# Sliding-window attention with an adaLN and SwiGLU block: the row-maximum products take 64 queries of both heads by a block-diagonal operand

## The chip, the cores and the metric

The kernel runs on one core of one Trainium2 chip. The metric is device time in microseconds (us) of one execution, from runs of the compiled program on the chip. A core has TensorE (PE, with its weight loads listed as PEld), VectorE (DVE), ScalarE (ACT), GpSimd (POOL) and SyncE (SP), which here only issues transfers; 16 DMA engines move the data.

## The reference

One transformer block on x of 2048 rows by 512, in float32. A vector c gives six modulation rows. Cut to what matters:

```
mod = silu(c) @ w_mod                       # sa, ca, ga, sb, cb, gb
h = layernorm(x) * (1 + ca) + sa
q, k, v = h @ wqkv                          # 32 heads of 16
scores = q @ k.T * 16 ** -0.5               # key index in (query - 256, query]
x = x + ga * (softmax(scores) @ v) @ wo
h = layernorm(x) * (1 + cb) + sb
out = x + gb * ((silu(h @ w1) * (h @ w3)) @ w2)
```

The softmax is over a window of 256 keys that ends at the query itself. This case is about the maximum over those keys, which is subtracted ahead of the exponential.

## The kernel before

**Tiling.** The sequence is cut into 4 blocks of 512 positions (`NB`, `BT`), the 32 heads into 8 groups of four (`NQ`). A unit is one group on one block, so there are 32 units, numbered u = 4 g + b. A unit's four heads are two pairs: index `a` picks one, and `hh` the head within it. Values that need more than one product's precision are held as high and low parts, so a projection is three products per chunk of 128 rows.

Each unit goes through three functions, and the three work on different units at the same time:

- `unit_a` (line 442) computes queries and keys: 12 products of 512 columns (line 451) into one bank `pj`, three ScalarE copies out of it (lines 457, 460 and 463), and two subtractions on GpSimd (`mix`, line 469) that leave three parts of each value. Then six transfers of 128 KB (`rows`, line 474) put the parts into `ring`, the operand memory in which one head's values have 48 rows (16 elements by three parts) and two heads have 96.
- `unit_b` (line 491) finds the row maximum: 16 products (line 504), each of 128 queries of one head against up to 384 keys. The stationary operand holds both heads' query rows (96 by 128), and the keys come from a copy of `ring` in which the other head's rows are zero. For each product VectorE adds the mask `mskq` and takes the maximum (line 511) and reads the accumulator. Then come `parts` (lines 519 and 520), a transpose (line 526), a ScalarE copy (line 531), and two small transfers `ring<-mT` (line 535) that put the negated maxima into extra rows of the query operand, so that the score product subtracts them itself.
- `unit_c` (line 743) makes 16 score products with keys as the stationary operand and up to 384 queries as columns (line 763), masks and exponentiates them, and multiplies by the values into the bank `po` (`values_of`, line 739). `MODE` gives each of the eight (key block j, pair a) one of the ways to mask: C merges the two partly masked blocks on VectorE (line 781), takes the exponential of 256 columns (line 784) and zeroes what is outside on GpSimd (line 791); D adds the mask on VectorE (line 771) and takes the exponential of 384 columns (line 775); P copies two blocks to a tile `sm` on ScalarE (line 798), takes the exponential of the free block (line 800), masks on GpSimd (line 808) and takes the exponential of the rest (line 812).

Score, row-maximum and projection products have three, three and one PSUM bank; `po` has one.

**Order.** Nothing is scheduled by the compiler. Every step is put on a list with a time, and each engine gets its steps in the order of those times; an engine does them in that order and waits where an operand is not there. The times are in slots: unit u begins at slot 8 u, `unit_a` of unit u at 8 (u - 3) + `oa`, `unit_b` at 8 (u - 2) + `ob`, and the dictionary `X` holds each step's place within its function. In every unit's eight slots there are therefore the projections of one unit, the maxima of an earlier one and the probabilities of one before that. SP also issues a store of the output bank (line 831), the loads and stores of a side job for the later feed-forward weights (lines 893 and 894; GpSimd does its arithmetic), and in every fourth unit the load of the next group's projection weights (line 432, split on lines 436 and 440) and a gate row (line 875).

Ahead of the units stand the modulation, the layer norm and the values of all blocks, with the first units by the plain times `Y`. The last units are merged by a planner (`Sched`) with the output projection and the feed-forward, which is TensorE products from end to end.

Of the kernel before, what the change touches and what calls it, by code (L numbers as in the profile page):

```python
# [17 lines left out]
H, DH = 32, 16  # L18
# [11 lines left out]
X = dict(oa=-1.228, ob=1.317, wqk=(-2.382, 3.131, 4.551), pj=(-1.966, -1.918, -1.881, -0.877, -0.359, -0.355,  # L30
         -0.265, 0.076, 1.497, 3.335, 3.917, 4.363), ev=(4.727, 5.775, 5.259), mix=(5.588, 6.021),
         row=(8.681, 8.806, 9.018), mx=(0.546, 0.669, 1.455, 2.0, 2.064, 2.307, 2.929, 2.957, 3.255, 4.081,
         4.688, 5.039, 6.139, 6.215, 6.787, 7.106), tl=(0.31, 0.576, 0.39, 0.716, 0.354, 0.742, 0.497, 1.151,
         0.762, 0.785, 0.491, 0.953, 0.338, 1.726, 1.317, 1.105), mr=(8.575, 8.773, 9.063, 9.269), st=(1.873,
         1.594, -2.503, 2.891, 0.05, 3.409, 2.644, 3.504, 4.618, 4.477, 4.419, 5.916, 5.311, 7.665, 6.691,
         6.671), c=(0.385, 0.805, 2.402, 0.573, 0.759, 1.126), pv=(4.115, 8.948, 9.091, 9.582, 3.792, 4.101),
         o=(9.93, 10.63), job=(-0.855, 2.493, 10.058))
Y = dict(wqk=(0, 4, 5), pj=(0.0, 0.382, 0.764, 1.146, 1.528, 1.91, 2.292, 2.674, 3.056, 3.438, 3.82, 4.202),
         ev=(4.991, 4.614, 4.813), mix=(5.389, 5.444), row=(5.416, 5.471, 6.776), mx=(0.0, 0.5, 1.0, 1.5,
# [3 lines left out]
MODE = 'CDCPCCCP'  # L43
# [259 lines left out]
def block_kernel(ctx: ExitStack, tc: tile.TileContext, x, wqk, wv, wo, w13, w2, c, wmod, out):  # L303
# [5 lines left out]
    ident = cst.tile([P, P], F32, name="ident")  # L309
    make_identity(nc, ident)  # L310
    nhalf = cst.tile([P, 4], F32, name="nhalf")
    nc.gpsimd.memset(nhalf, -0.5)
    o32 = cst.tile([P, P], F32, name="o32")
    nc.gpsimd.memset(o32, 1.0 / 32)
    odd = cst.tile([P, 1], F32, name="odd")

    def fill_odd():

        for hh in range(2):
            r = slice(64 * hh, 64 * hh + 64)  # L320
            nc.vector.tensor_reduce(
                out=odd[r], in_=ident[r].rearrange("p (c o) -> p c o", o=4)[:, :, 2 - 2 * hh:4 - 2 * hh],
                op=ALU.add, axis=mybir.AxisListType.XY)
        nc.vector.tensor_copy(identr, ident)
# [61 lines left out]
    ring = ap.tile([P, 3, 2, S], F32R, name="ring")  # L386

    NS, NM = 6 * DH, 6 * DH + 4

    def queries(rows, a, b, n):  # L390
        return ring[:rows, 1, a, b * P:(b + n) * P]

    def keys(rows, hh, a, b, n):
        return ring[:rows, 2 - 2 * hh, a, b * P:(b + n) * P]


    mskq = ap.tile([P, 3 * P], F32, name="mskq")
    nc.gpsimd.memset(mskq, 0.0)
    nc.gpsimd.affine_select(out=mskq[:, :P], in_=mskq[:, :P], pattern=[[1, P]], base=0,
                            channel_multiplier=-1, compare_op=ALU.is_gt, fill=NEG)  # L400
    nc.gpsimd.affine_select(out=mskq[:, 2 * P:], in_=mskq[:, 2 * P:], pattern=[[-1, P]], base=0,
                            channel_multiplier=1, compare_op=ALU.is_ge, fill=NEG)
    mskw = a1.tile([P, KC, P], F32, name="wqr", bufs=1)
    mskk = mskw[:, :2]
# [7 lines left out]
    identr = ap.tile([P, P], F32R, name="identr")  # L412
# [7 lines left out]
    def ring_fill(b, hh):  # L420
        k = ring.bitcast(F32)[:, 2 - 2 * hh, :, b * BT:(b + 1) * BT]
        nc.gpsimd.memset(k[:NM] if hh == 0 else k[:NS], 0.0)
        if hh:
            nc.gpsimd.memset(k[NS:NM], 1.0)
        nc.gpsimd.memset(k[NS:NS + 2], 1.0 - hh)
# [16 lines left out]
    def unit_a(u, t0, at, y=X):  # L442
# [11 lines left out]
        def out(n):  # L454
            if n == 0:
                v["raw"] = a1.tile([P, BT], F32, name="qkr", bufs=1)
                nc.scalar.activation(v["raw"], v["ps"], AF.Copy)  # L457
            elif n == 1:
                v[0] = a1.tile([P, BT], F32R, name="qk0", bufs=1)
                nc.scalar.activation(v[0], v["ps"], AF.Copy)  # L460
            else:
                v[1] = a1.tile([P, BT], F32R, name="qk1", bufs=1)
                nc.scalar.activation(v[1], v["ps"], AF.Copy, scale=odd)

        def mix(n):

            if n == 2:
                v[2] = a1.tile([P, BT], F32R, name="qk2", bufs=1)
            nc.gpsimd.tensor_tensor(out=v[n], in0=v["raw"], in1=v[1].bitcast(F32), op=ALU.subtract)  # L469

        def rows(r):
            rf = ring.bitcast(F32)
            for hh in range(2):
                nc.sync.dma_start(
                    rf[3 * hh + r:NS:6, 1 - hh:3 - hh, :, b * BT:(b + 1) * BT].rearrange(
                        "p x a t -> p (x a) t"),
                    v[r].bitcast(F32)[64 * hh:64 * hh + 64, :])
# [10 lines left out]
        for r in range(3):  # L488
            at(t0 + y["row"][r], lambda r=r: rows(r), "qk_rows")

    def unit_b(u, t0, at, y=X):
# [4 lines left out]
        def scores(i):  # L496
            qb, a, hh = i // 4, i // 2 % 2, i % 2
            gq = 4 * b + qb
            k0 = max(0, gq - 2)
            n = (gq + 1 - k0) * P  # L500
            if i == 0:
                v["mt"] = a1.tile([P, 2, 2, 4], F32, name="mt", bufs=2)
            v[i] = psA.tile([P, BT], F32, name="mx", bufs=MXB)
            nc.tensor.matmul(v[i][:, :n], queries(NS, a, gq, 1), keys(NS, hh, a, k0, gq + 1 - k0),  # L504
                             start=True, stop=True)

        def top(i):
            qb, a, hh = i // 4, i // 2 % 2, i % 2
            n = min(3, 4 * b + qb + 1) * P
            junk = a1.tile([P, 3 * P], BF16, name="junk", bufs=2)  # L510
            nc.vector.tensor_tensor_reduce(  # L511
                out=junk[:, :n], in0=v[i][:, :n], in1=mskq[:, 3 * P - n:], scale=1.0, scalar=-3e38,
# [1101 lines left out]
```

## Time and profile before

| | |
|---|---|
| runs | 969.67, 972.69 and 973.76 us; median 972.69 us |
| the profiled execution, first to last instruction | 971.3 us, 1.4 us under that median |
| TensorE busy | 942.4 us, of it the row-maximum products 154.9 us and the score products 155.3 us |
| VectorE busy | 734.9 us, of it the maximum over the row-maximum products 256.3 us |
| ScalarE and GpSimd busy | 557.1 and 538.2 us |
| DMA | 80672 packets, 141.65 MB |

Busy times are sums over instructions; on TensorE they overlap, since a product starts before the one ahead of it has drained. How far apart products start is therefore read from the chain of work that ended last, in which neighbours on one engine are counted from start to start. A line that starts with "L504 PE" is one group of instructions: line of the kernel, engine, operation, what is written and read, shapes and count, then busy time, mean duration in ns, and idle time ahead of them with its releaser.

### The profile page before, as it was taken

The page shows a single profiled execution, that of the slowest core. Times are in us where ns is not written, and L with a number is a line of the kernel's source. Part 1 is how long each engine was busy: PE and PEld are TensorE (multiplying, and loading weights), DVE is VectorE, ACT ScalarE, POOL GpSimd, SP SyncE. Part 2 cuts the span into 40 slices and gives each one's busy share as a digit, 9 for nine tenths or more (in the row PEclk, how much of TensorE's full clock was granted, in tenths as well). Part 3 has the DMA queues.
Part 4 walks back from the last instruction along what each step waited for, and adds up shares of the span by engine and source line. Part 5 has one row for each costly group of instructions (what it writes and reads, how often), then busy time and mean ns, then how long its engine had stood idle before and what let it go on. Part 6 is the DMA issues. An engine that isn't in the chain of part 4 may idle for free.

```text
span 971.3 us, 17150 instructions
## 1 busy us (share of the span) xinstructions
PE 942.4 (97%) x5316; PEld 717.5 (74%) x5316; DVE 734.9 (76%) x2034; ACT 557.1 (57%) x1258; POOL 538.2 (55%) x740
## 2 busy tenths in 40 slices
PE   6999999999999999998998999999999999999998
PEld 3678777777767776775577888888887888888886
DVE  7575889998989998999278686666679766677545
ACT  3333878787878787876578843433456343433330
POOL 8321777787868786865546765337759332222320
PEclk9999999999999999999898999999999999999999
DMA  9521354444544444435795564467654433222102
GB/s 317 170 77 36 134 182 143 144 143 144 176 143 143 144 144 143 133 128 174 211 243 139 194 217 151 142 206 249 194 195 165 141 119 94 63 65 72 44 23 87
DMA packets 80672, 141.65 MB, mean 146 GB/s; under 512 B 9538, under 2 KB 22338, under 8 KB 80580
## 3 DMA queue, kind: packets, MB, share of 16 engines
q1 hardware_dynamic: 79860, 139.50, 44.6%
q10 hardware_dynamic: 720, 1.05, 0.3%
q8 instruction: 42, 0.69, 0.3%
q14 instruction: 50, 0.41, 0.1%
HBM read 85.72 MB, written 34.61 MB: 124 GB/s over the span
## 4 chain that ended last, share of the span: by engine, by line
PE 83%; POOL 5%; DVE 4%; DMA 3%; issue 2%; ACT 2%; SPq 1%; POOLq 0%; DVEq 0%; ACTq 0%
PE st L1384 13%; PE mx L1384 11%; PE pj L451 7%; PE mx L504 7%; PE mx L1478 7%; PE st L763 7%; PE st L1478 7%; PE po L739 6%; PE pj L1384 5%; PE st L671 3%; PE pj L1478 2%; PE mx L1120 2%; POOL pt L791 2%; PE st L1120 2%; POOL qk L469 2%
## 5 line engine op out<-in xcount | busy, mean ns | idle before, releaser
L511 DVE CUSTOM_DVE_ANT_0 junk<-mx,mskq 128x384 bf16<-128x384 f32 (+2 forms) x512 | 256.3, 527 | 28.8 <-PE mx L504 27.2
L504 PE MATMUL mx<-ring 96*128 96x384 f32 (+2 forms) x512 | 154.9, 340 | 6.0 <-DMA ring<-qk 2.4
L763 PE MATMUL st<-ring 100*128 100x384 f32 (+2 forms) x512 | 155.3, 345 | 2.2 <-ACT pt L784 1.2
L791 POOL TENSOR_SCALAR_AFFINE_SELECT pt<-pt 128x256 f32<-128x256 f32 x268 | 109.3, 411 | 63.1 <-ACT pt L784 52.5
L451 PE MATMUL pj<-hT,wq 128*128 128x512 f32 x384 | 136.2, 404 | 1.2 <-DVE wq L440 0.8
L504 PEld LDWEIGHTS mx<-ring 96*128 96x128 f32 x512 | 93.5, 189 | 39.7 <-DVE mt L511 25.8
L784 ACT ACTIVATE pt<-st 128x256 f32<-128x256 f32 x268 | 96.1, 386 | 41.8 <-DVE st L781 33.8
L763 PEld LDWEIGHTS st<-ring 100*128 100x128 f32 x512 | 95.5, 190 | 23.7 <-issue 8.4
L739 PE MATMUL po<-pt,vS 128*17 128x384 f32 (+2 forms) x1408 | 98.6, 398 | 1.7 <-POOL pt L791 1.0
L469 POOL TENSOR_TENSOR qk<-qkr,qk 128x512 fp32r<-128x512 f32 x64 | 83.3, 1302 | 27.6 <-ACT qkr L457 27.4
L976 POOL TENSOR_TENSOR w<-w,w 128x512 fp32r<-128x512 f32 (+2 forms) x36 | 59.8, 1679 | 62.0 <-ACT w L975 44.6
L1428 POOL TENSOR_TENSOR t<-t,t 128x512 f32<-128x512 f32 x28 | 39.7, 1418 | 93.5 <-DVE t L1416 91.7
L781 DVE COPY_PREDICATED st<-later,st 128x128 f32<-128x128 uint8 x268 | 72.2, 291 | 17.4 <-PE st L763 14.5
L451 PEld LDWEIGHTS pj<-hT,wq 128*128 128x128 f32 x384 | 71.4, 190 | 10.2 <-issue 1.7
L739 PEld LDWEIGHTS po<-pt,vS 128*17 128x17 f32 x1408 | 33.5, 98 | 48.4 <-issue 22.4
L1384 PE MATMUL st<-b,w 128*128 128x512 f32 x258 | 64.1, 390 | 0.0
L775 ACT ACTIVATE pt<-st 128x384 f32<-128x384 f32 (+2 forms) x128 | 52.7, 434 | 18.8 <-DVE st L771 12.4
L1416 DVE TENSOR_TENSOR t<-st,t 128x512 f32<-128x512 f32 x52 | 35.7, 686 | 36.4 <-PE st L1384 31.2
L808 POOL TENSOR_SCALAR_AFFINE_SELECT sm<-sm 128x256 f32<-128x256 f32 x109 | 42.1, 409 | 27.9 <-ACT sm L798 25.2
L1456 ACT ACTIVATE wq<-g 128x512 fp32r<-128x512 f32 x28 | 17.8, 634 | 67.5 <-PE st L1478 40.7
L1384 PE MATMUL mx<-b,w 128*128 128x512 f32 x222 | 56.0, 390 | 0.0
L1384 PEld LDWEIGHTS st<-b,w 128*128 128x128 f32 x258 | 48.4, 188 | 10.2
(270 smaller groups left out, 2083.1 us busy)
## 6 DMA issues: line engine op xcount, KB each, us to landing
ring<-qk SPq DMA_DIRECT2D x192, 128.0 KB
o_dr<-os SPq DMA_DIRECT2D x32, 256.0 KB
w<-wsum SPq DMA_DIRECT2D x14, 512.0 KB
w<-w2g SPq DMA_DIRECT2D x14, 512.0 KB
jb<-in_w SPq DMA_DIRECT2D x24, 256.0 KB
wraw<-in_w SPq DMA_DIRECT2D x7, 768.0 KB
w<-wraw SPq DMA_DIRECT2D x14, 384.0 KB
vS<-in_wmod SPq DMA_DIRECT2D x20, 256.0 KB
```

What stands on the lines that cost most here:

```text
L451: nc.tensor.matmul(v["ps"], WQ[g][w][:, n // 3], hTp(i, n // 3, b * BT, BT), start=(n == 0), stop=(n == 3 * KC - 1))
L469: nc.gpsimd.tensor_tensor(out=v[n], in0=v["raw"], in1=v[1].bitcast(F32), op=ALU.subtract)
L504: nc.tensor.matmul(v[i][:, :n], queries(NS, a, gq, 1), keys(NS, hh, a, k0, gq + 1 - k0), start=True, stop=True)
L511: nc.vector.tensor_tensor_reduce(out=junk[:, :n], in0=v[i][:, :n], in1=mskq[:, 3 * P - n:], scale=1.0, scalar=-3e38, op0=ALU.add, op1=ALU. ...
L739: nc.tensor.matmul(po[32 * i:32 * i + DH + 1, qb * P:(qb + nq) * P], vS[:, kb, 4 * g + i], pts[i // 2][:, i % 2, c0:c0 + nq], start=first, ...
L763: nc.tensor.matmul(ps[:, :nq], keys(NM, hh, a, kb, 1), queries(NM, a, kb, nq), start=True, stop=not plus)
L781: nc.vector.copy_predicated(ps[:, 0], later, ps[:, 2])
L784: nc.scalar.activation(held[u, j, a][:, hh, :2], v[j, a, hh][:, :2], AF.Exp, scale=SCALE)
L791: nc.gpsimd.affine_select(out=pt[:, :, 2 * m], in_=pt[:, :, 0], **w)
L976: sch.op(eng, lambda: on_eng(eng).tensor_tensor(out=lo(), in0=src(), in1=hi().bitcast(F32), op=ALU.subtract), tt(eng, n), key, kl + kh, kl ...
L1384: nc.tensor.matmul(ps(bk), WT[s, n][w][:, col], BB[t, k][r], start=start and c == 0, stop=stop and c == 5, skip_group_check=True)
L1478: nc.tensor.matmul(ps(bk), tiles[hk + (h,)][:, i * P:(i + 1) * P], w2_of(last, y, f), start=(m == 0), stop=(m == 5))
```

## The change

A row-maximum product now takes 64 queries of both heads of a pair at once. Queries stand in `qring` as [rows, pair, chunk of 64, head, 64], with zeros in the rows of the other head, so that the 128 columns of one chunk are a block-diagonal stationary operand; keys stand once, in `kring`, with both heads' rows. 64 queries need at most 5 chunks of 64 keys, so a product has up to 320 columns in place of 384, and there are still 16 in a unit.

- The six transfers of `rows` go to a staging tile `qk2` (queries) and to `kring` (keys). A new step `spread` sends the queries on from the staging tile into `qring`: four transfers of 96 KB whose rows are written in pieces of 64 values, 256 bytes each.
- The score product reads its columns from `qring` in pieces of 64 that stand 128 apart, and has 98 rows in place of 100. The negated maxima go to two rows in place of four.
- In `MODE` the fourth entry is D where it was P, in all but the last three units. The remaining P works inside `pt`, without `sm`.
- The third part of queries and keys is written over `qkr`; `junk` has one buffer in place of two.
- The places in `X` are new for every step. `ident`, `odd`, the masks and the filling of constant rows are set up by other instructions ahead of the units.

```diff
-MODE = 'CDCPCCCP'
+MODE = 'CDCDCCCP'
...
-    ring = ap.tile([P, 3, 2, S], F32R, name="ring")
...
+    kring = ap.tile([P, 2, S], F32R, name="kring")
+    qring = ap.tile([P, 2, S // HP, 2, HP], F32R, name="qring")
...
         def rows(r):
-            rf = ring.bitcast(F32)
+            if r == 0:
+                v["qt"] = a1.tile([P, 2, BT], F32R, name="qk2", bufs=1)
+            for x, to in enumerate((v["qt"], kring[:, :, b * BT:(b + 1) * BT])):
+                nc.sync.dma_start(to.bitcast(F32)[r:NS:3], v[r].bitcast(F32)[HP * x:HP * x + HP, :])
+
+        def spread():
             for hh in range(2):
-                nc.sync.dma_start(
-                    rf[3 * hh + r:NS:6, 1 - hh:3 - hh, :, b * BT:(b + 1) * BT].rearrange(
-                        "p x a t -> p (x a) t"),
-                    v[r].bitcast(F32)[64 * hh:64 * hh + 64, :])
+                h = slice(NS // 2 * hh, NS // 2 * hh + NS // 2)
+                for a in range(2):
+                    nc.sync.dma_start(qring.bitcast(F32)[h, a, 8 * b:8 * b + 8, hh],
+                                      v["qt"].bitcast(F32)[h, a].rearrange("p (c q) -> p c q", q=HP))
...
-            nc.tensor.matmul(v[i][:, :n], queries(NS, a, gq, 1), keys(NS, hh, a, k0, gq + 1 - k0),
+            nc.tensor.matmul(v[i][:, :n * HP], pair(NS, a, c), keys(NS, a, (c + 1 - n) * HP, n * HP),
                              start=True, stop=True)
...
-                out=junk[:, :n], in0=v[i][:, :n], in1=mskq[:, 3 * P - n:], scale=1.0, scalar=-3e38,
-                op0=ALU.add, op1=ALU.max, accum_out=v["mt"][:, a, hh, qb:qb + 1])
+                out=junk[:, :n * HP], in0=v[i][:, :n * HP], in1=mskq.rearrange("p c k -> p (c k)")[:, (5 - n) * HP:],
+                scale=1.0, scalar=-3e38, op0=ALU.add, op1=ALU.max, accum_out=v["mt"][:, a, c:c + 1])
...
-            nc.tensor.matmul(ps[:, :nq], keys(NM, hh, a, kb, 1), queries(NM, a, kb, nq),
+            nc.tensor.matmul(ps[:, :nq], keys(NM, a, kb * P, P), queries(NM, hh, a, 2 * kb, 2 * nq),
                              start=True, stop=not plus)
```

Of the places in `X`, those that the prediction speaks of:

| step | before | after |
|---|---|---|
| `oa`, start of `unit_a` | -1.228 | -2.303 |
| last product, `pj` | 4.363 | 1.286 |
| `row`, three steps of two transfers | 8.681, 8.806, 9.018 | 4.438, 4.628, 4.768 |
| `bd`, the spread | none | 6.715 |
| `ob`, start of `unit_b` | 1.317 | 0.242 |
| first product, `mx` | 0.546 | 0.503 |
| last of `mr`, the maxima's transfers | 9.269 | 9.992 |

More of the change, by code (lines that the diff above doesn't have):

```diff
@@ L411, in block_kernel @@
     mskr = ap.tile([P, 2, P], F32R, name="mskr")
-    identr = ap.tile([P, P], F32R, name="identr")
     def fill_masks():
@@ L733, in block_kernel, with pv @@
     held = {}
-    def pv(kb, g, pts, qb, c0, nq, first, last):
+    def pv(kb, g, pts, qb, c0, nq, first):
         for i in range(4):
@@ L820, in values_of @@
             here = min(nq, 4 - j)
+            first = "pv" not in v
             if uu == u:
-                pv(kb, g, pts, j, 0, here, b == 0 and j == 0, j == 3)
+                v["pv"] = True
+                pv(kb, g, pts, j, 0, here, first)
             elif nq > here:
-                pv(kb, g, pts, 0, here, nq - here, j == 2, False)
+                v["pv"] = True
+                pv(kb, g, pts, 0, here, nq - here, first)
         def out():
```

119 lines of the change are left out of this document (57 added, 62 removed).

## The prediction, made blind

> **What bounds the kernel now.** I read the page first (span, busy times, the chain that ended last), then one wide window of the main stage, then the chain in order of time.
>
> ```profile
> span 971.3 us, 17150 instructions
> PE 942.4 (97%) x5316; PEld 717.5 (74%) x5316; DVE 734.9 (76%) x2034; ACT 557.1 (57%) x1258; POOL 538.2 (55%) x740
> ...
> PE 83%; POOL 5%; DVE 4%; DMA 3%; issue 2%; ACT 2%; SPq 1%; POOLq 0%; DVEq 0%; ACTq 0%
> ```
>
> The chain lies on TensorE for 83% of the span. The change touches the attention units, so the window of 100 to 400 us matters (PE, PEld, DVE, ACT, POOL with counts, the granted clock, DMA share, GB/s), and the same window for the row-maximum products alone:
>
> ```profile
> 100.00:400.00 300.00, 294.06 (x2216) 213.29 (x2215) 271.46 (x1153) 236.97 (x671) 227.83 (x418) 1.00 0.45 148
> 100.00:400.00 300.00, 119.96 (x401) 73.09 (x401) 1.00 0.45 148
> ```
>
> 401 products, 16 to a unit, are 25.06 units in 300 us: 11.97 us a unit, and a slot of the schedule is an eighth of it, 1.50 us. VectorE is busy 271.46 / 25.06 = 10.83 us of a unit, ScalarE 9.46, GpSimd 9.09; the granted clock is 1.00. Now the chain (start, length, what), from one transpose of the maxima (L526) to later ones:
>
> ```profile
> 182.46 0.11 PE mx L526
> ...
> 194.09 0.11 PE mx L526
> ...
> 200.28 0.35 PE mx L504 x2
> 200.63 0.70 PE pj L451 x3
> ...
> 205.67 0.11 PE mx L526
> ...
> 206.78 0.23 PE pj L451
> ...
> 217.43 0.11 PE mx L526
> ...
> 219.27 0.81 POOL wq L440
> ...
> 229.66 0.11 PE mx L526
> ```
>
> The reader should see that from 182.46 to 217.43 the distances are 11.63, 11.58 and 11.76 us, on TensorE nearly without a break: about 11.55 us is TensorE's work in a unit. The last distance, 12.23 us, has a stretch on GpSimd (the split of projection weights at 219.27). So of 11.97 us a unit about 0.42 us is waiting, and TensorE sets the pace. It also shows what a column costs: 0.175 us for a product of 384 columns and 0.233 us for one of 512, so (0.233 - 0.175) / 128 = 0.456 ns a column. The 349 ns that the groups give overlap and are no price.
>
> **The change, part by part.** *Row-maximum products.* 384 to 320 columns saves 64 x 0.456 = 29 ns a product, 0.467 us in a unit of 16. In the first block of each group the old products have 4 x 128, 4 x 256 and 8 x 384 columns, 4608, the new ones 2 x (64 + 128 + 192 + 256) + 8 x 320 = 3840: 768 columns, 0.350 us. Units 2 to 28 run in the main stage: 20 x 0.467 + 7 x 0.350 = 11.8 us. The other five stand in the mixed first and last stages; of their 2.2 us I count half, 1.1 us. Ends: 0 and 14.0 us. Could the weight load hold a product at its old length?
>
> ```profile
> 80.15 0.44 PE st L649 x4
> ```
>
> Transposes with a full 128-column operand come every 0.11 us, so a product of 0.146 us can follow.
>
> *VectorE, ScalarE, GpSimd.* By form, 100 to 400 us:
>
> ```profile
> L511 DVE CUSTOM_DVE_ANT_0 junk<-mx,mskq 128x384 bf16<-128x384 f32 x354 | 185.7, 552 | 14.0 <-PE mx L504 12.9
> ...
> L469 POOL TENSOR_TENSOR qk<-qkr,qk 128x512 fp32r<-128x512 f32 x50 | 64.7, 1293 | 0.0
> ...
> L808 POOL TENSOR_SCALAR_AFFINE_SELECT sm<-sm 128x256 f32<-128x256 f32 x94 | 36.3, 409 | 23.4 <-ACT sm L798 20.7 <-DMA ring<-qk 2.7
> L798 ACT ACTIVATE sm<-st 128x256 f32<-128x256 f32 x89 | 34.0, 382 | 0.8
> ...
> L812 ACT ACTIVATE pt<-sm 128x512 f32<-128x512 f32 x44 | 28.1, 639 | 0.4
> ...
> L800 ACT ACTIVATE pt<-st 128x128 f32<-128x128 f32 x88 | 25.0, 284 | 0.0
> L775 ACT ACTIVATE pt<-st 128x384 f32<-128x384 f32 x50 | 24.5, 491 | 0.3
> L771 DVE TENSOR_TENSOR st<-st,mskr 128x256 f32<-128x256 f32 x50 | 21.4, 427 | 0.0
> ...
> L511 DVE CUSTOM_DVE_ANT_0 junk<-mx,mskq 128x256 bf16<-128x256 f32 x24 | 10.1, 422 | 6.4 <-PE mx L504 6.1
> ```
>
> 128 columns of the maximum cost 552 - 422 = 130 ns, so 64 save 65 ns, 1.04 us a unit. The fourth entry of MODE, P to D, adds two masks, 0.85 us. VectorE falls by 0.19 us to 10.64 us, but of a unit of 11.5 us that is 92.5%, where it was 90.5%. ScalarE loses 2 x 382 + 2 x 284 + 639 and gains 2 x 491 ns: 0.99 us less. GpSimd loses 2 x 409 ns. None of the three is on the chain for long, so I count their relief as nothing (TensorE's 11.1 us hides it), and for VectorE's tighter fit I charge 0.05 us a unit, 1.3 us; ends 0 and the second rival's.
>
> *The spread.* It is the one new cost. SyncE in one unit, and a transfer of more pieces:
>
> ```profile
> 209.88 3.90 SPq L474 DMA_DIRECT2D ring<-qk  x6
> 213.82 0.59 SPq L894 DMA_DIRECT2D wsum<-jb  x1
> 218.07 1.40 SPq L535 DMA_DIRECT2D ring<-mT  x2
> 219.52 0.43 SPq L831 DMA_DIRECT2D o_dr<-os  x1
> ...
> 539.12 0.56 SPq L897 DMA_DIRECT2D wraw<-in_w  x1
> ```
>
> An issue takes 0.65 us with six, and 0.56 us where it has 512 pieces (768 KB in pieces of 1536 bytes), so pieces don't lengthen it. Four more issues are 2.6 us. SyncE's work, with 0.4 us for the job's load, goes from 6.7 to 9.3 us, and it waits for the staged rows to land ahead of the spread, an estimated 0.9 us: 10.2 of 11.5 us. Behind the waiting spread stand the next job load, the job store, the next unit's rows and its maxima; GpSimd's job waits for the first, TensorE for the last two.
>
> The latency decides. Today:
>
> ```profile
> 211.27 1.29 POOL L469 TENSOR_TENSOR qk<-qkr,qk 128x512 fp32r<-128x512 f32 x1
> ```
>
> The last projection product starts at 206.78, the second mix ends at 212.56, the sixth transfer is issued at 213.78: 7.0 us, 7.9 us with the landing. The new chain adds 2.6 us of issue and 1.0 us until the last lands: 11.5 us. In the places, last product to first row-maximum product is 8.745 + 1.017 = 9.76 slots (6.73 before), 14.0 us at 1.44 us a slot. So 2.5 us are to spare, and I cost the spread at nothing.
>
> What could eat these 2.5 us is the price of a 256-byte packet. There are 4 x 384 = 1536 in a unit, 96 on each of 16 engines.
>
> ```profile
> q1 hardware_dynamic: 79860, 139.50, 44.6%
> ...
> DMA packets 20, 0.01 MB, mean 5 GB/s; under 512 B 4, under 2 KB 20, under 8 KB 20
> ...
> q1 hardware_dynamic: 20, 0.01, 1.9%
> ```
>
> The page's mean packet, mostly 2 KB, takes 0.446 x 16 x 971.3 / 79860 = 87 ns. The last two lines are 218.0 to 219.6 us, where only the maxima's 512-byte pieces move: 0.019 x 16 x 1.6 / 20 = 24 ns. Ends 0 and 87 ns; I take 24 ns, nearest in size. Then an engine is busy 2.3 us more a unit, beside 0.446 x 11.97 = 5.3 us, and the issue hides it.
>
> The Trainium skill speaks against the change here: its page "DMA: Bandwidth & Descriptors", section Specifications, asks for at least 512 bytes for full rate and has smaller writes done as read-modify-write; the section "Why small descriptors are slow (HBM only)" exempts transfers within SBUF. No trace here shows 256-byte data. By the first section the first rival would decide, by the second this sum stands.
>
> *The maxima's transfers.* They now stand behind the first two row transfers, at slot 2.23; the first score product that needs them stands at 3.05 (2.59 and 4.42 before). 0.82 slots are 1.2 us, the two issues 1.4 us. But SyncE runs ahead of its places:
>
> ```profile
> SPq L535 <- ACT pt L784: 83.4, 22, 5.4
> ```
>
> It stood idle ahead of these transfers 22 times, 3.8 us each, so I take 0; were it never ahead, 0.3 us x 27 = 8 us.
>
> *The rest.* The weight split on GpSimd now stands after both mixes (slot 3.32 against 1.82 and 2.38) and not ahead of them (3.32 against 4.36), which can only shorten the wait of every fourth unit; ends 0 and 0.42 us x 27 = 11 us, taken as 0. Score products keep count and columns; reading them in pieces of 64 has no row, and I take 0. One `junk` buffer is written and dropped by VectorE alone, in order: 0. The feed-forward stays as it is: 0.
>
> *Sum.* 11.8 + 1.1 - 1.3 = 11.6 us: 971.3 becomes 959.7. The profiled execution lies 1.4 us under the median of 972.69, so **961.0 us**.
>
> **The rivals.**
>
> *The spread is late (slower).* The schedule forces a unit to last at least chain x 8 / 9.76. With p ns a packet the spread takes 96 p where that exceeds 2.6 us. It binds from a chain of 14.0 us, p = 53 ns; from 59 ns the unit is at its old 11.97 us. At 70 ns, midway from 53 to 87, the chain is 15.6 us, the unit 12.8, and 0.83 x 27 = 22 us are lost: 995 us. At 87 ns it is 1031 us. For it: 1536 packets are 1.6 times what a unit has now (79860 over the whole run is under 1000 per unit's length), and a shared queue. Against: 24 ns. Chance 0.18; 0.02 more for pieces of 64 that slow the score products, at any price upward.
>
> *VectorE becomes the pace.* It is idle 1.14 us a unit now, and TensorE's weight loads wait for it:
>
> ```profile
> PEld mx L504 <- DVE mt L511: 18.2, 37, 0.6
> ```
>
> If it needs the same 1.14 us beside its 10.64, a unit is 11.78 us: 0.19 x 27 = 5 us gained, 967.5 us; with a little more waiting it is no change. Against: TensorE itself, not its loads, rarely waits for it. Chance 0.16.
>
> *The columns don't set the time.* Then 972 us; the transposes speak against it. Chance 0.02.
>
> *The new order also removes waits.* Half of 0.42 us x 27 is 5.7 us: 955 us, or less. Chance 0.10.
>
> **How the numbers follow.** The forecast has 0.52, with its own range of 956 to 967 us. Under 0.5%, 4.9 us, a measurement of this kernel can't tell a change from none. Faster: 0.52 + 0.10 = 0.62. Same: 0.16 + 0.02 = 0.18. Slower: 0.20. The range goes from 952, past the last rival's price, to 984, about a third into the first; it leaves out some 0.14 above and 0.03 below.
>
> **What would show it.** Right: L526 to L526 near 11.1 to 11.2 us within TensorE stretches, pairs of row-maximum products 0.29 us on the chain, the 320-column maximum near 487 ns, DMA share near 0.65, and no wait of a row-maximum product for the spread. Wrong: such waits in every unit, or VectorE on the chain between products; packets of the spread over 53 ns; score products over 0.175 us apart.

## The result, and the profile after

The changed kernel takes **1012.52 us** (median of 4 runs, 1010.28 to 1017.13) against 973.23 us of the kernel before on the same chip (969.67 to 977.51): a ratio of 1.0405, 95% interval 1.0365 to 1.0444. The forecast was 961.0 us, with 952 to 984 as its range. The profiled execution spans 1015.4 us, 44.1 us more than the one of before.

The page of the changed kernel: span, busy times, shares of the chain that ended last.

```profile
span 1015.4 us, 17270 instructions
...
PE 953.0 (94%) x5316; PEld 711.1 (70%) x5316; DVE 742.9 (73%) x2091; ACT 535.6 (53%) x1171; POOL 505.7 (50%) x673
...
PE 70%; DVE 19%; ACT 3%; issue 3%; DMA 2%; POOL 1%; SPq 1%; DVEq 0%; ACTq 0%; POOLq 0%
```

VectorE is busy only 8 us more than before (742.9 against 734.9), and yet it holds 19% of the chain where it held 4%. Busy time alone does not show why. The window of 100 to 400 us of the changed kernel, all instructions and then the row-maximum products alone:

```profile
100.00:400.00 300.00, 276.37 (x2030) 193.05 (x2029) 256.64 (x1097) 203.12 (x550) 193.63 (x344) 0.98 0.70 166
100.00:400.00 300.00, 116.10 (x367) 70.41 (x367) 0.98 0.70 166
```

367 products are 22.9 units in 300 us, 13.1 us a unit where the kernel before had 12.0 and the forecast wanted about 11.5. The granted clock of the window is 0.98 where it was 1.00; two per cent of TensorE's 11.55 us in a unit are 0.2 us, and e2 below loses 23 us with 1.00 in the same window. VectorE's idle time is hidden in its timeline (start, length, what) between neighbouring maxima. First before, then after:

```profile
203.50 0.55 DVE L511 CUSTOM_DVE_ANT_0 junk<-mx,mskq 128x384 bf16<-128x384 f32 x1
203.97 0.09 DVE L511 DVE_READ_ACCUMULATOR2_ANT mt<- 128x1 f32 x1
203.97 0.56 DVE L511 CUSTOM_DVE_ANT_0 junk<-mx,mskq 128x384 bf16<-128x384 f32 x1
```

```profile
204.20 0.49 DVE L513 CUSTOM_DVE_ANT_0 junk<-mx,mskq 128x320 bf16<-128x320 f32 x1
204.61 0.08 DVE L513 DVE_READ_ACCUMULATOR2_ANT mt<- 128x1 f32 x1
204.84 0.49 DVE L513 CUSTOM_DVE_ANT_0 junk<-mx,mskq 128x320 bf16<-128x320 f32 x1
```

Before, a maximum starts 0.47 us after its neighbour, while the one ahead (0.55 us) is still draining. After, it is shorter (0.49 us) but starts 0.64 us after its neighbour: it has to wait until that one has ended. Both write the tile `junk`, of which the change left one buffer.

To see where the 44.1 us lie I cut each profiled execution at the first and the last store of an attention unit's output (start, length, SyncE's issue). Before, then after:

```profile
113.21 0.43 SPq L831 DMA_DIRECT2D o_dr<-os  x1
...
488.73 0.33 SPq L831 DMA_DIRECT2D o_dr<-os  x1
```

```profile
123.16 0.53 SPq L833 DMA_DIRECT2D o_dr<-os  x1
...
523.22 0.33 SPq L833 DMA_DIRECT2D o_dr<-os  x1
```

So 10.0 us are lost ahead of the first store, 24.5 us between the stores (375.5 to 400.1), and 9.6 us behind the last one (482.6 to 492.2). The prediction put all of the change but 1.1 us between the stores.

### The profile page after: what moved, and what is told of

It reads as the page before. It is cut to its first block, busy times and chain, and to the rows that moved or that the text cites. A ratio compares the mean times of both kernels' runs of the same rounds, so it can differ in the third digit from the quotient of the medians.

```text
span 1015.4 us, 17270 instructions
## 1 busy us (share of the span) xinstructions
PE 953.0 (94%) x5316; PEld 711.1 (70%) x5316; DVE 742.9 (73%) x2091; ACT 535.6 (53%) x1171; POOL 505.7 (50%) x673
## 4 chain that ended last, share of the span: by engine, by line
PE 70%; DVE 19%; ACT 3%; issue 3%; DMA 2%; POOL 1%; SPq 1%; DVEq 0%; ACTq 0%; POOLq 0%
PE st L1386 11%; PE mx L1386 11%; DVE junk L513 9%; PE mx L1480 7%; PE st L764 6%; PE pj L451 6%; PE st L1480 6%; PE mx L506 5%; PE po L740 4%; PE pj L1386 4%; PE st L672 3%; PE pj L1480 2%; DVE st L782 2%; DVE mr L520 1%; PE mx L1122 1%
## 5 line engine op out<-in xcount | busy, mean ns | idle before, releaser
L513 DVE CUSTOM_DVE_ANT_0 junk<-mx,mskq 128x320 bf16<-128x320 f32 (+3 forms) x512 | 239.5, 468 | 48.6 <-PE mx L506 7.8
L764 PE MATMUL st<-qring,kring 98*128 98x384 f32 (+2 forms) x512 | 162.5, 363 | 8.3 <-DMA qring<-mT 3.4
L506 PE MATMUL mx<-kring,qring 96*128 96x320 f32 (+3 forms) x512 | 163.3, 330 | 6.4 <-DVE mt L513 3.5
L451 PE MATMUL pj<-hT,wq 128*128 128x512 f32 x384 | 148.0, 405 | 2.2 <-ACT wq L436 1.6
L506 PEld LDWEIGHTS mx<-kring,qring 96*128 96x128 f32 x512 | 98.2, 192 | 39.3 <-DVE mt L513 22.9
L764 PEld LDWEIGHTS st<-qring,kring 98*128 98x128 f32 x512 | 95.7, 195 | 39.9 <-ACT pt L785 13.1
L776 ACT ACTIVATE pt<-st 128x384 f32<-128x384 f32 (+2 forms) x186 | 77.6, 447 | 37.8 <-DVE st L772 24.9
L467 POOL TENSOR_TENSOR qk<-qkr,qk 128x512 fp32r<-128x512 f32 x32 | 41.2, 1288 | 79.0 <-ACT qkr L458 57.7
L772 DVE TENSOR_TENSOR st<-st,mskr 128x256 f32<-128x256 f32 (+1 forms) x162 | 55.9, 386 | 3.2 <-PE st L764 3.2
L1418 DVE TENSOR_TENSOR t<-mx,t 128x512 f32<-128x512 f32 x47 | 32.3, 687 | 31.2 <-PE mx L1386 25.1
```

What stands on the lines that cost most here:

```text
L451: nc.tensor.matmul(v["ps"], WQ[g][w][:, n // 3], hTp(i, n // 3, b * BT, BT), start=(n == 0), stop=(n == 3 * KC - 1))
L506: nc.tensor.matmul(v[i][:, :n * HP], pair(NS, a, c), keys(NS, a, (c + 1 - n) * HP, n * HP), start=True, stop=True)
L513: nc.vector.tensor_tensor_reduce(out=junk[:, :n * HP], in0=v[i][:, :n * HP], in1=mskq.rearrange("p c k -> p (c k)")[:, (5 - n) * HP:], sca ...
L764: nc.tensor.matmul(ps[:, :nq], keys(NM, a, kb * P, P), queries(NM, hh, a, 2 * kb, 2 * nq), start=True, stop=not plus)
L776: nc.scalar.activation(held[u, j, a][:, hh, :nq], v[j, a, hh][:, :nq], AF.Exp, scale=SCALE)
L1418: return nc.vector.tensor_add(o, x, y)
```

## The experiments

Times are medians of 4 runs in each case, ratios are against the kernel before on the same chip. Diffs are against the changed kernel unless said otherwise.

### One junk buffer, and the spread

e1: the changed kernel with two buffers (in another pool, since the first had no room for a second).

```
-            junk = a1.tile([P, 5 * HP], BF16, name="junk", bufs=1)
+            junk = ap.tile([P, 5 * HP], BF16, name="junk", bufs=2)
```

> The changed kernel with two buffers for the output of the maximum (junk) in place of one; they lie in the attention pool. Theory A, the single junk buffer: a maximum that directly follows another waits until that one has written its last column. In the changed kernel neighbours start 0.645 us apart where one separated by other work needs 0.415 us; some 10 of 16 in a unit are such neighbours, 2.3 us, which makes VectorE's 10.6 us into the 12.7 us that a unit lasts. A expects neighbours 0.42 us apart, units of 11.2 to 11.8 us, and 960 to 985 us. Theory B, the spread and the fuller transfer queue (rows and maxima land late): no change, 1005 to 1015 us. Theory C, VectorE is the pace with its own work alone, the maxima's spacing being set by the 320-column reading: no change either.

e2: the kernel before with one.

```
-            junk = a1.tile([P, 3 * P], BF16, name="junk", bufs=2)
+            junk = a1.tile([P, 3 * P], BF16, name="junk", bufs=1)
```

> The kernel before with one junk buffer in place of two, nothing else. Theory A: neighbouring maxima go from 0.475 to about 0.71 us apart; with about 8 neighbours a unit VectorE gets 1.9 us more, units of 12.5 to 13 us, 985 to 1003 us. Theories B and C: within 3 us of the kernel before.

e3 and e4: the line that places the spread is left out, with one junk buffer and with two; query rows then stay zero.

```
-        at(t0 + y["bd"], spread, "qk_rows")
```

> The changed kernel without the four spread transfers of a unit; the query rows of the operand stay zero, so maxima and scores are not those of the reference. Theory A: 1003 to 1015 us, the units stay at 12.6 us. Theory B: the loss goes, 960 to 980 us.

> Two junk buffers and no spread transfers (query rows zero, so maxima and scores are not those of the reference). Theory A: within 5 us of the run with two junk buffers alone, since the spread is covered. If the spread costs something once VectorE no longer hides it, 5 to 20 us less than that run.

| run | time, us | ratio, interval |
|---|---|---|
| e1, two junk buffers | 993.43 | 1.0247, 1.0229 to 1.0264 |
| e2, before with one | 993.15 | 1.0236, 1.0220 to 1.0251 |
| e3, no spread | 1008.09 | 1.0391, 1.0375 to 1.0406 |
| e4, no spread, two junk buffers | 977.32 | 1.0074, 1.0059 to 1.0089 |

One buffer costs the kernel before 23.4 us. The changed one it costs 15 (by the ratios) to 19 us (by the times), and 30.8 us when the spread is left out (e3 against e4). Theory A had the mechanism, but e1 lies 8 us above its range: the buffer is not all of the loss. The timeline of e1 shows the wait gone:

```profile
203.42 0.49 DVE L513 CUSTOM_DVE_ANT_0 junk<-mx,mskq 128x320 bf16<-128x320 f32 x1
203.83 0.08 DVE L513 DVE_READ_ACCUMULATOR2_ANT mt<- 128x1 f32 x1
203.83 0.49 DVE L513 CUSTOM_DVE_ANT_0 junk<-mx,mskq 128x320 bf16<-128x320 f32 x1
```

and that of e2 shows it made, in a kernel with no other edit:

```profile
204.58 0.56 DVE L511 CUSTOM_DVE_ANT_0 junk<-mx,mskq 128x384 bf16<-128x384 f32 x1
205.06 0.08 DVE L511 DVE_READ_ACCUMULATOR2_ANT mt<- 128x1 f32 x1
205.29 0.56 DVE L511 CUSTOM_DVE_ANT_0 junk<-mx,mskq 128x384 bf16<-128x384 f32 x1
```

The maxima start 0.41 us apart in e1 for 0.64, and 0.71 in e2 for 0.47. In the changed kernel 226 of 365 maxima between 100 and 400 us are followed by another one, ten to a unit, so the waiting is 10 x 0.23 = 2.3 us a unit, 62 us in 27 units. Only part of that reaches the end; that the rest falls into time in which VectorE would have been idle is an inference, not shown.

The spread costs 1 (by the ratios) to 4 us (by the times) while VectorE is held by `junk` (e3), and 16 to 17 us when it isn't (e4 against e1): one cost was hidden by the other.

### The columns alone

e7: the kernel before with 320 columns in products and maxima, and with scores scaled by a quarter.

```
+            cut = max(0, n - 320)
-            nc.tensor.matmul(v[i][:, :n], queries(...), keys(...),
+            nc.tensor.matmul(v[i][:, :n - cut], queries(...), keys(...)[:, cut:],
-            n = min(3, 4 * b + qb + 1) * P
+            n = min(320, (4 * b + qb + 1) * P)
```

> The kernel before, with its row-maximum products and maxima cut from 384 to the last 320 columns. It leaves 64 keys out of every maximum, and the scores are scaled by a quarter so that nothing overflows; number and shape of all other instructions stay. Theory (TensorE's columns set the unit's time, 29 ns a product, as the prediction's first term has it): 11 to 13 us less than before, 957 to 959. Rival (other engines are already as close, so that a third or more of the columns' gain comes back as waiting): 961 to 966. Second rival: the columns don't set the time: 968 to 972.

960.58 us, ratio 0.9901 (0.9869 to 0.9933): 9.9 us less, the interval says 6.5 to 12.7. That lies between the ranges of the theory and of the first rival, and the interval holds the 11.8 us of the sum's first term, so its size stands. As e7 shortens VectorE's maxima with TensorE's products, it doesn't tell whose columns those were.

### MODE, and the places

e8: before, with `MODE = 'CDCDCCCP'`.

> The kernel before with the fourth entry of MODE from P to D: 0.85 us more VectorE in a unit, 0.99 us less ScalarE, 0.82 us less GpSimd, nothing else changed. By the prediction's rule (VectorE is idle 1.14 us in a unit of 11.97; if it needs the same idle time beside 10.83 + 0.85 us, a unit is 12.82 us): 0.85 x 27 = 23 us more, 990 to 996. Rival (VectorE still fits into TensorE's unit, since ScalarE and GpSimd are relieved): 968 to 974. Between the two, 975 to 989: part of the masks lies on the path.

996.34 us, ratio 1.0284 (1.0248 to 1.0321). One entry costs 25.9 us, about the 23 us that the theory has. What TensorE waited for, 110 to 440 us (total, times, longest), has a line that the kernel before doesn't have:

```profile
PE st L763 <- ACT pt L775: 15.2, 25, 0.7
```

A score product waits for its bank, which is released by an exponential that stands behind a mask, which stands behind maxima in VectorE's order. These waits are 15.2 us of the 25.9; the run doesn't part them from VectorE's greater work as such.

e9: e1 with P back.

> The changed kernel with two junk buffers and the fourth entry of MODE back to P. In the kernel before, D in that place alone cost 25.9 us (a run above). Theory (the masks on VectorE, and score buffers that wait for a mask behind row maxima in VectorE's order, cost about as much in the new places): 15 to 25 us less than the 993.4 with two junk buffers and D: 968 to 978. Rival (the new places were laid out for D, VectorE's work there stands apart from the score products, and P's own transfers through GpSimd meet the subtractions instead): 988 to 1000.

990.81 us, ratio 1.0189 (1.0145 to 1.0232). My expectation failed: in the new places D costs at most a few us, 2.6 by the times and 5.6 by the ratios, whose intervals just touch.

e13 and e14: the kernel before with all new places, with D and with P (`X`, `Y` and `MODE` as in the change's diff, no new product, mask or transfer). Two things follow the new order as in the change: the value product that comes first in a unit opens the bank, and in e14 P works inside `pt`.

> The kernel before with the change's places and its MODE (D), nothing else of the change; its order of the value products' first start follows the new places, as in the change. Theory (the new places cost time by themselves: the first store 5 to 8 us later, the stage behind the last store 8 to 11 us longer, and D about 20 us between): 985 to 1015, with the first store at 118 to 121 us and 490 to 494 us behind the last store. Rival (the places are as good as the old ones and the loss belongs to the new code): 968 to 980 with the first store near 113 and 481 to 484 us behind the last.

> The run above with P in the fourth entry of MODE; P masks its probabilities in place as in the change, because the extra buffer with the new places would deadlock. Theory (places cost 15 to 19 us outside the main stage, MODE little in the new places as it did in the changed kernel): within 5 us of the run above, and 980 to 1000. Rival (D is what costs, as with the old places): 20 us or more under the run above.

990.53 us (ratio 1.0185, 1.0146 to 1.0224) and 992.20 us (1.0198, 1.0162 to 1.0234). **The new places alone cost 17 to 19 us**, with either mode. The stores of e13:

```profile
118.57 0.55 SPq L834 DMA_DIRECT2D o_dr<-os  x1
...
494.03 0.33 SPq L834 DMA_DIRECT2D o_dr<-os  x1
```

5.4 us are lost ahead of the first store and 9.8 us behind the last (span 986.4); between them it takes 375.5 us, as before. VectorE is nearly full there (125 to 425 us), but taking 0.85 us a unit off it (e14) changed nothing that can be told, and TensorE waited as long at the transpose of the maxima (110 to 440 us; 0.9 us in the kernel before). E13, then e14's line of waits:

```profile
125.00:425.00 300.00, 283.62 (x2201) 213.56 (x2194) 289.43 (x1185) 215.24 (x588) 204.75 (x361) 1.00 0.45 146
...
PE mx L526 <- DVE mr L520: 15.2, 20, 0.8
```

```profile
PE mx L526 <- DVE mr L520: 15.0, 20, 0.8
```

e15 and e16: the changed code with two junk buffers and P, and the old places of maxima, score and value products, or all the old places.

> The changed code with two junk buffers and P, its projections, subtractions, row transfers and spread at the new places, but row-maximum products, maxima, score products, value products, stores and jobs at the places of before. Theory (the tight order of VectorE's work in the new places is what eats the columns' gain): 965 to 980. Rival (the lead of the projections, which stays, makes start and end longer, and the spread's load stays): 985 to 1000.

> The changed code with two junk buffers and P at the places of before throughout, the spread right behind the row transfers (place 9.05). From the last projection product to the first row-maximum product there are 6.73 slots, and the chain through the spread took 11.5 us in the prediction's sum. Theory (the distance sets the pace: 11.5 x 8 / 6.73 = 13.7 us a unit): start and end as in the kernel before, the main stage 45 to 60 us longer: 1010 to 1035. Rival (the chain is shorter than its sum or overlaps more, so that the old places would have done): 965 to 985.

1044.15 us (1.0730, 1.0688 to 1.0773) and 1085.89 us (1.1166, 1.1121 to 1.1212). With all the old places the spread is too late: a chain longer than its distance, as in the prediction's first rival, but from the distance and not from the price of a packet. TensorE in e16 (110 to 440 us, as for e15 below):

```profile
PE mx L499 <- DMA qring<-qk: 44.6, 18, 4.0
```

My model of chain by slots was too kind, e16 lies 50 us above its upper end. E15 lies above both of its ranges. Its projections waited for ScalarE's copies instead:

```profile
PE pj L444 <- ACT qk L454: 22.9, 23, 1.1
```

Both tell one thing more. The stores of e16:

```profile
120.23 0.39 SPq L826 DMA_DIRECT2D o_dr<-os  x1
...
601.51 0.33 SPq L826 DMA_DIRECT2D o_dr<-os  x1
```

Behind the last store it takes 1084.7 - 601.5 = 483.2 us, as before, with all the new code in it. In every kernel with the new places of the products this stage takes 490 us or more. E15, whose last store starts at 563.55 us of 1044.6, has 481.0; e9, which differs from it in the places of maxima, score and value products alone, has 492.4. A long stage between the stores is not the reason, since e5 below has 501.0 us there and still 493.7 behind. So the 10 us at the end belong to those places. Some 6 of them are waits: TensorE waits 9.0 us behind the last store of e13 and 2.8 in the kernel before, and the new waits are for VectorE and ScalarE, among them 3.1 us for a feed-forward weight (L1387) and 2.3 us for the output projection's operand (L1123), which neither e15 nor e16 shows. Ahead of the first store the old places gain nothing back in the new code: it comes at 124.4 us in e15 and at 120.2 in e16.

### The transpose, GpSimd, and the maxima's transfers

In e1 TensorE still waits, and for two things above all (110 to 440 us). The last line is its wait for the spread; the third names the spread too, but the transpose (L527) reads nothing of it, so what it waited for is not known:

```profile
PE mx L527 <- DVE mr L521: 10.4, 17, 0.9
PE st L764 <- DMA qring<-mT: 8.8, 11, 1.4
PE mx L527 <- DMA qring<-qk: 1.3, 2, 0.8
PE mx L506 <- DMA qring<-qk: 0.9, 2, 0.6
```

e10: e1 with the transpose and its copy placed later. e11: that with P. e12: e11 with the maxima's transfers issued by ScalarE.

```
-mr=(8.099, 8.425, 8.463, 9.992)
+mr=(8.099, 8.85, 8.9, 9.992)
-                nc.sync.dma_start(qring.bitcast(F32)[NS:NM, ...   (e12 only)
+                nc.scalar.dma_start(qring.bitcast(F32)[NS:NM, ...
```

> The changed kernel with two junk buffers and the places of the maxima's transpose and of its cut moved from 8.425 and 8.463 to 8.85 and 8.9, 0.6 us later in TensorE's order, so that other products run while VectorE's two small operations end. Theory (TensorE stands 0.6 us a unit at this transpose because it is in order, and nothing needs the transpose so early): the 10.4 us that it waited for them in 330 us go, the time falls by 8 to 14 us from 993.4: 979 to 985. Rival (the maxima's transfers come later by the same time and the score products wait for those instead of TensorE for the transpose): 990 to 997.

> Both of the two edits above: two junk buffers, P, and the later transpose. Theory (two causes that don't overlap): the sum of both gains, 20 to 37 us under 993.4: 956 to 973; under 967 it beats the kernel before. Rival (both take away the same waiting on VectorE): as the better of the two alone, 970 to 985.

> The run above, with the maxima's two transfers issued by ScalarE in place of SyncE, so that they don't stand behind the first two row transfers. Theory (8.8 us of waiting for the maxima's transfers come from SyncE's order): 5 to 8 us less than the run above. Rival (the transfers share the DMA engines with the rows and the spread, and issues on ScalarE delay its exponentials): the same within 2 us, or up to 10 us more.

990.87 us (1.0191, 1.0155 to 1.0226), 994.70 us (1.0234, 1.0200 to 1.0269) and 1038.59 us (1.0671, 1.0623 to 1.0719). E10 gains 2.6 us by the times, 5.4 by the ratios, where its theory has 8 to 14: the wait left the transpose and came back one step on. E10 (110 to 440 us):

```profile
PE mx L506 <- DVE mt L513: 8.2, 18, 0.6
```

A row-maximum product waits for its bank until VectorE has taken a maximum, so moving the transpose buys little. E11 misses its sum of two gains, and e12 lies 44 us above e11, outside both of its ranges: the score products wait 32.9 us there for the maxima's transfers (110 to 440 us; 5.5 in e11). Why they land later from ScalarE was not followed.

e5: e1 with the two subtractions placed later on GpSimd. Unintended, the first now stands behind the row transfer of its own tile, so that pair of transfers carries the values ahead of the subtraction.

```
-mix=(4.127, 4.68)
+mix=(4.66, 4.7)
```

> The changed kernel with two junk buffers, and the places of GpSimd's two query/key subtractions moved from 4.127 and 4.68 to 4.66 and 4.7, so that the part in GpSimd's masks goes first and the two small operations that negate the maxima (parts, VectorE) don't meet the first subtraction. Theory (VectorE's small operations with two SBUF operands are held while GpSimd's 1.29 us subtraction runs, and TensorE's transpose waits for them): the two operations fall from 1.11 us together to about 0.45 us, the transpose's wait of 0.9 us in 17 of some 27 units mostly goes, and the time falls by 5 to 15 us from 993.4: 978 to 988. Rival (the two lengths only coincide, or the wait moves to the next operation): 990 to 996. Second rival: the later subtractions make the spread late: over 996.

1125.55 us (1.1596, 1.1555 to 1.1637), and GpSimd's waits (125 to 425 us) name the reason: the subtraction waits until the transfers have read its tile.

```profile
POOL qk L467 <- DMA kring<-qk: 117.2, 18, 7.9
```

So the run says nothing of the theory that it was for, only what 6.5 us of delay in the chain to the spread cost.

e6: e1 with the maxima's transfers ahead of the first row transfers (`mr[3]` 9.85).

> The changed kernel with two junk buffers, and the place of the maxima's two transfers moved from 9.992 to 9.85, ahead of the first two row transfers on SyncE. Theory (with VectorE no longer late, the maxima's transfers stand behind two row transfers on the queue of issues and share the DMA engines with them and the spread, so that score products wait for them, 8.8 us in all in the window of 100 to 440 us): that wait goes, the time falls by 5 to 8 us from 993.4: 985 to 989. Rival (the rows and with them the spread come 1.4 us later, and the first row-maximum products wait instead): 992 to 1000.

1000.86 us (1.0317, 1.0278 to 1.0356): the rival, just past its range. The score products' wait for the maxima falls from 8.8 to 2.6 us (110 to 440 us), but the row-maximum products now wait 8.3 us for the spread, 0.9 in e1.

### What of the spread costs

In e1 SyncE's first row transfer of a unit waits for the staging tile, which the spread of the unit ahead is still reading, and the maxima's transfers stand behind it (125 to 425 us):

```profile
SPq L473 <- DMA qring<-qk: 16.0, 27, 1.6
```

e17: e1 with an eighth of each spread transfer. e18: e1 with the key transfer ahead of the query transfer in the first pair.

```
-  nc.sync.dma_start(qring.bitcast(F32)[h, a, 8 * b:8 * b + 8, hh], v["qt"].bitcast(F32)[h, a]...
+  nc.sync.dma_start(qring.bitcast(F32)[h, a, 8 * b:8 * b + 1, hh], v["qt"].bitcast(F32)[h, a, :HP]...
```

```
+            both = list(enumerate((v["qt"], kring[:, :, b * BT:(b + 1) * BT])))
-            for x, to in enumerate((v["qt"], kring[:, :, b * BT:(b + 1) * BT])):
+            for x, to in both[::-1] if r == 0 else both:
```

> The changed kernel with two junk buffers, whose four spread transfers move only the first of the eight groups of 64 queries each (192 packets a unit for 1536); the other groups stay zero in the products, everything else stays. Theory (packets: their 2 to 3 us on the DMA engines hold the staging buffer and delay the row and maxima transfers): 10 us or more come back, 977 to 983. Rival (issues: SyncE has 2.65 us more to issue whatever moves): 989 to 995.

> The changed kernel with two junk buffers, where of the first two row transfers of a unit the one of the keys is issued first and the one of the queries, which waits for the staging buffer, second. Theory (the wait for the staging buffer stands ahead of the maxima's transfers, and TensorE waits 8.8 us for those): 0.5 us of SyncE a unit goes, 3 to 8 us in all: 985 to 990. Rival (the query transfer comes 0.6 us later, the maxima's transfers stay behind it): 991 to 997.

984.09 us (1.0140, 1.0114 to 1.0165) and 988.14 us (1.0190, 1.0155 to 1.0225). Without most of its packets the spread costs 6.4 us (1.0140 against e4's 1.0074, of 971), with them 16.8. So some 10 us go with the data that moves and 6 with the rest of the step, its four issues among it; by the intervals either can be some 3 us off. The line of waits above falls from 16.0 to 0.3 us in e17 and to 2.5 in e18. E18 gets 5 us back without moving less, so that part belongs to where SyncE waits for the staging tile. TensorE's waits in e18 show only some of it: those of score products for the maxima fall from 8.8 to 6.5 us (110 to 440 us). No version of the changed kernel that computes everything beats the kernel before; e18, e9 and e10 come nearest, each at a ratio of 1.019.

## Why the prediction was wrong

**The account by stages.** Four profiled executions lie between before and after. The stores of e4 and of e1 give the two that are still missing:

```profile
119.65 0.53 SPq L832 DMA_DIRECT2D o_dr<-os  x1
...
482.74 0.33 SPq L832 DMA_DIRECT2D o_dr<-os  x1
```

```profile
121.19 0.53 SPq L833 DMA_DIRECT2D o_dr<-os  x1
...
494.58 0.33 SPq L833 DMA_DIRECT2D o_dr<-os  x1
```

| step to | first store at | between the stores | behind the last | span | step |
|---|---|---|---|---|---|
| before | 113.2 | 375.5 | 482.6 | 971.3 | |
| new places, D (e13) | 118.6 | 375.5 | 492.4 | 986.4 | +15.1 |
| new code and columns, no spread, two junk (e4) | 119.7 | 363.1 | 493.4 | 976.1 | -10.3 |
| spread (e1) | 121.2 | 373.4 | 493.4 | 988.0 | +11.9 |
| one junk buffer (after) | 123.2 | 400.1 | 492.2 | 1015.4 | +27.4 |

The ratios give the same signs with other sizes: +18, -11, +17 and +15 us (differences of the ratios, times 971). The last two differ because e1's profiled run (989.68 us) lies 4 us under its median and that of after (1017.13) 5 us over; their sum, 32 to 39, is firmer than its parts. The order of the steps matters too: the spread is 16 to 17 us with two buffers and 1 to 4 with one, and the second buffer is worth 15 to 19 us with the spread and 30.8 without it. No one term carries the loss: with two buffers the kernel still takes 993.43 us, outside the range.

**The step that failed.** "One `junk` buffer is written and dropped by VectorE alone, in order: 0." An engine that does its work in order doesn't wait for order, but in these kernels VectorE does wait for the end of a write to the same tile, and that end lies 0.08 us behind the point at which the next one could start (0.49 against 0.41 us in e1); until the waiting one really starts another 0.15 us pass (0.64 against 0.49): 0.23 us for each neighbour. E1 and e2 show it in both directions. The second rival, VectorE as the pace, thus came true in part (19% of the chain), but by a wait that counts as no busy time: the prediction looked for it in busy time (92.5%), found room, and priced it at 967.5 us.

The Trainium skill, page "VectorE: DVE Perf Modes", section "The DRAIN you can't avoid", has the next operation start when the pipe is empty, and earlier where it is not held; in its measurement of eight copies a semaphore after each cost nothing. Here neighbours without a wait do start early (0.41 us apart at 0.49 us each, e1), which agrees, and those with one don't (0.64 us). So a wait has a price here that it hadn't in that measurement, and by that measurement the 0 would have stood as well.

**The spread at nothing** failed next, 12 to 17 us. Its price of a packet was nearly right: while the spread moves (201.75 to 205.3 us of the changed kernel) the trace has

```profile
DMA packets 1420, 0.49 MB, mean 139 GB/s; under 512 B 1338, under 2 KB 1338, under 8 KB 1420
...
q1 hardware_dynamic: 1420, 0.49, 64.0%
```

0.64 x 16 x 3.55 = 36.4 us of engine time; less 82 larger packets at the 87 ns of the prediction, 1338 take 21.8 ns each, where 24 was taken. The first rival, which needed 53 ns, didn't come about by its price. The distance was long enough too: with the new one the row-maximum products waited 0.9 us in all for the spread in e1, with the old one 44.6 us (e16). What the sum left out, in part at least, is the single staging tile: the next unit's first query transfer waits until the spread has read it, and "the next unit's rows and its maxima", named there as standing behind, were costed at nothing. "SyncE runs ahead of its places" holds far less in the new code: SyncE's idle time ahead of the maxima's transfers is 98 us in the kernel before, 32 in e4 and 16 in e1 (125 to 425 us). E17 puts 10 us on the data and 6 on the rest of the step, and e18 some 5 on the tile; beyond that the cause stays open.

**Nothing for the ends** failed as well, and it is as large as the other two: 15 to 18 us. The sum has half of 2.2 us for them, "The feed-forward stays as it is: 0", and no word on what other places do there: +5.4 us ahead of the first store, +9.8 us behind the last (e13). That it is the places of maxima, score and value products which make the end longer is shown by e9 against e15. How they do so is open: some 6 us are new waits of TensorE, and the planner writes the output projection's order around those places, but I made no run that changes only that. What delays the first store is open too.

**P to D, at 0.85 us of VectorE less 1.04.** In the old places the entry costs 25.9 us (e8), in the new ones nothing that can be told between e13 and e14 and at most a few us between e1 and e9. That the sum came out right there is partly luck: it reckoned with VectorE's total, and the same total costs 25.9 us in other places. Whether a mask stands between a score product and its bank is what e8's waits point to; it is not shown by itself.

**What held.** The columns: 11.8 us between the stores forecast, 12.4 measured from e13 to e4 (375.5 to 363.1, the rest of the new code included), 9.9 in e7. In both cases the maxima got shorter with the products, and VectorE was 96% busy in e13, so the size held, but how much of it is TensorE's was not tested apart. A 320-column maximum takes 489 ns, where 487 were expected, and the DMA share is 0.70 for 0.65.

## What to carry to other kernels

Count the buffers of every output tile, also of one that nobody reads: where neighbouring VectorE instructions wrote the same tile, as here, the overlap of each with the next was gone with one buffer and there with two, and busy time didn't show it. When a step gets a staging tile, ask when the next round may write it and what is queued behind that transfer. When a schedule's places move, cost the beginning and the end of the pipeline as a term of its own, and test it by putting the new places into the old kernel.

## What the runs showed of the hardware

VectorE's small operations on SBUF can take as long as a GpSimd operation that runs beside them. E1, VectorE and then GpSimd, twice:

```profile
198.42 1.19 DVE L520 TENSOR_SCALAR mr<-mt 128x16 fp32r<-128x16 f32 x1
...
211.20 1.13 DVE L521 SCALAR_TENSOR_TENSOR mr<-mt,mr 128x16 fp32r<-128x16 f32 x1
```

```profile
198.31 1.27 POOL L467 TENSOR_TENSOR qk<-qkr,qk 128x512 fp32r<-128x512 f32 x1 [3.85 <-ACT qkr L458]
...
210.98 1.31 POOL L467 TENSOR_TENSOR qk<-qkr,qk 128x512 fp32r<-128x512 f32 x1 [0.31 <-ACT qkr L458]
```

Both end within 0.04 us of GpSimd's subtraction (199.61 and 199.58, 212.33 and 212.29). Of 28 units between 100 and 440 us, 21 have such a long operation; in the other seven GpSimd's subtraction starts some 0.1 us after the second of the two. In the kernel before, seven of 28 units have one of 0.99 to 1.29 us, each beside a product of 128x512 of the side job (L880). Beside the side job's operations of 128x128 both take 0.17 us:

```profile
204.57 0.17 DVE L519 TENSOR_SCALAR mr<-mt 128x16 fp32r<-128x16 f32 x1
204.78 0.17 DVE L520 SCALAR_TENSOR_TENSOR mr<-mt,mr 128x16 fp32r<-128x16 f32 x1
```

```profile
204.25 2.10 POOL L889 TENSOR_TENSOR jb<-jb 128x128 f32<-128x128 f32 x4
```

The Trainium skill, page "SBUF — State Buffer", section "Who interferes with whom", has a port pair that the two engines hold by turns, for a whole instruction each, when VectorE reads two SBUF inputs or runs in a mode that uses both ports. The rows of e1 agree with it, those of the kernel before show that not every GpSimd operation beside them does this, and no run here tells what sets the 128x128 ones apart. What that wait is worth in the kernel's time stays open as well: e5 was meant to tell and didn't, and when the transpose was moved out of its way (e10) the gain was 3 to 5 us.
